# Issuing the loads of later tokens and of the first raw weights behind named stores

## The chip, the cores and the metric

The kernel runs on one core of a Trainium2 chip. A core has four engines that compute, each with its own instruction stream: TensorE (PE in the profile, its weight loads as PEld), VectorE (DVE), ScalarE (ACT) and GpSimdE (POOL). SyncE (SP) issues transfers. A transfer is carried out by the core's 16 DMA engines, and whoever needs its data or its buffer waits for a semaphore. The metric is the device time of one execution in microseconds (us), as a median over runs.

## What is computed

Tokens `x` (2048 x 448, float32) are layer-normalised to `xn`. The output is the sum of three terms: `x`, an attention over `xn`, and a gated feed-forward layer over `xn`.

```python
x = A_x
xn = layernorm(x)
return x + A_ref(xn, wq, wk, wv, wo, beta) + B_ref(xn, w_gate, w_up, w_down)

# A_ref: 16 heads of 28, 4 segments of 512 tokens, one after the other
logits = einsum("bhqd,bhkd->bhqk", qs, ks) * scale + mask
a_dot = softmax(logits) @ vs
a_mem = (phi(qs) @ M) / (phi(qs) @ z + 1e-6)    # phi(t) = t + 1 if t > 0 else exp(t)
o = g * a_mem + (1 - g) * a_dot                 # g = sigmoid(beta), one per head
M = M + phi(ks).T @ vs
z = z + sum(phi(ks))
# then o @ wo

# B_ref
h = sigmoid(xn @ w_gate) * (xn @ w_up)
return h @ w_down
```

So each segment reads the memory `M`, `z` that the segments before it have filled, and attends within itself.

## The kernel before

**Blocks.** The 2048 tokens are worked on in four blocks of 512 (`b` = 0 to 3 in the code, block one to four in the text), which are also the segments. `acc[b]` holds a block's tokens and later collects the output; `xs[b]` holds the normalised, transposed tokens as a high and a low part. Products of full precision are made of 11 TensorE products of such parts.

**The front** (lines 268 to 562) runs over the four blocks. For a block it

- multiplies the four groups of 128 tokens by the value weights (`values`, product `pv`), copies the result into `vst`, and stores that to DRAM as `vd[b]` (L332);
- in the first of these groups, takes the statistics of the *next* block's tokens on VectorE (`statistics`, L285 to L287), which is the first use of `acc[b + 1]`;
- multiplies by seven pieces of the key and query weights (`keys_queries`, product `pp` at L344), the pieces in step `k` = 0 to 6. ScalarE copies each result into a tile `qk` (L345) and makes `e`, that is phi of the keys or queries (L349, L350). VectorE adds the low part (L351), and SyncE stores the tile to `qd[b]` (L352). In later blocks phi of the queries goes to `fd[b]` as well (L357);
- turns phi of the keys with TensorE (`key_rows`, product `pk`, copied to `kn` by ScalarE at L366) and updates the memory (`update`, product `pmm` at L372). The product `pmm` of the first update uses the PSUM bank that the second `pk` used, so it comes after that copy at L366;
- normalises and turns the next block's tokens (`normalise`, and `turn` with the product `pt` at L95);
- reads the memory for the block before (`phi_queries` loads `phi` from `fd`, L383; `recall`, product `n` at L390).

The tiles `qk` come from a pool of four buffers, `four_k`. A fifth tile, and the tiles `hh` of the feed-forward, can be written only when the store of the one that had the buffer has landed. The first buffers of the pool are also used by the raw value weights and one raw piece of the key and query weights.

**The feed-forward** is a generator, `gated`. Each `next(ffn)` lets it issue a few instructions. Its first steps load the first raw weights (`load_up(0)`), split them into a high and a low part (`ready_up(0)`, L85 on ScalarE and L86 on VectorE, into `wgu`), and load the next ones (`load_up(1)`, `load_down(0)`). They are called in the front. Its TensorE products (`pgu` at L240, then `pd` at L166) begin in block four of the front. After the front the feed-forward runs on, and the attention within blocks (`Pair`, `Unit`, products `st` and `pa`) is woven between its steps; that part loads its keys and queries from `qd` (L580) and its values from `vd`.

**What sets the order.** In the front, TensorE, ScalarE and VectorE keep the order in which the code is written:

```python
FRONT = {mybir.EngineType.PE, mybir.EngineType.Activation, mybir.EngineType.DVE}
...
    with tc.tile_pool(name="front", bufs=2) as sb, tc.manual_schedule(engines=FRONT):
```

SyncE is not among them. Its order in the front is made by a scheduler when the program is built, which issues a transfer as soon as it thinks that the transfer is ready; a load into a buffer that nobody has used is ready at once. Within SyncE's queue the order is then fixed: an entry that waits holds up those behind it. After the front, TensorE and SyncE keep the order of the code.

Of the kernel before, what the change touches and what calls it, by code (L numbers as in the profile page):

```python
# [9 lines left out]
F32 = mybir.dt.float32  # L10
# [6 lines left out]
P = 128  # L17
# [44 lines left out]
def kernel(  # L62
# [10 lines left out]
    nc = tc.nc  # L73
# [8 lines left out]
    acc = [keep.tile([P, NT, D], F32, name=f"acc{b}") for b in range(NB)]  # L82
# [5 lines left out]
    def split_weights(w, raw):  # L88
        split(w[:, 0:4, :], w[:, 4:8, :], raw)
# [18 lines left out]
    def x_block(b):  # L108
        return x[b * L:(b + 1) * L, :].rearrange("(t p) d -> p t d", p=P)
# [5 lines left out]
    def bank(name, tag):  # L115
        return ps.tile([P, L], F32, name=name, tag=tag, bufs=banks[tag])
# [17 lines left out]
    qd = [dram.tile([2 * D, 2, L], F32, name=f"qd{b}") for b in range(NB)]  # L134
# [6 lines left out]
    def eight_k(dtype, name):  # L141
        return mid.tile([P, 8, 256], dtype, name=name, tag="8k")

    def four_k(dtype, name):
        return mid.tile([P, 2, L], dtype, name=name, tag="4k", bufs=4)
# [13 lines left out]
    def gated():  # L159
# [14 lines left out]
        def load_up(f):  # L174

            raw_up[f] = mid.tile([P, 1024], F32, name="raw", bufs=2)
            if f < NF:
                nc.sync.dma_start(raw_up[f], w_ffn[f][:, :1024])
            else:
                nc.sync.dma_start(raw_up[f][:, :2 * D], w_o[:, 2 * D * (f - NF):2 * D * (f - NF + 1)])  # L180

        def load_down(f, tag="rawd"):
            raw_down[f] = (mid.tile([P, 1024], F32, name="raw", bufs=2)[:, :D] if tag == "raw" else
                           mid.tile([P, D], F32, name="rawd", bufs=1))
            nc.sync.dma_start(raw_down[f], w_ffn[f][:, 1024:])

        def ready_up(f):
            wgu[f] = eight_k(F32R, "wgu")
            split_weights(wgu[f], raw_up[f].rearrange("p (c n) -> p c n", c=4))
# [10 lines left out]
        load_up(0)  # L200
        yield
        ready_up(0)
        load_up(1)
        load_down(0)
        yield
# [62 lines left out]
    with tc.tile_pool(name="front", bufs=2) as sb, tc.manual_schedule(engines=FRONT):  # L268
# [21 lines left out]
        def root(vh):  # L290
            y = sb.tile([P, vh.shape[1]], F32, name=f"y{vh.shape[1]}")
            A.activation(y, vh, AF.Sqrt, scale=-2.0)
            return y
# [26 lines left out]
        def turn(b, t, xn):  # L320
            transpose_split(bank("pt", "s"), xn, xs[b], t)
# [7 lines left out]
        def store_values(b, t, pv):  # L329
            A.activation(vst[:, t, :, :DH], pv[:, :D].rearrange("p (h d) -> p h d", d=DH), AF.Copy)  # L330
            if t == NT - 1:
                nc.sync.dma_start(vd[b], vst.rearrange("p t h d -> p t (h d)"))  # L332

        def values(b, t):
            pv = bank("pv", "p")
            value_terms(b, t, pv, EARLY[1] if b == 0 else TERMS)
            store_values(b, t, pv)

        def keys_queries(b, c):

            qk = four_k(F32R, "qk")
            pp = bank("pp", ("p", "gu" if b < NB - 1 else "s")[c % 2])
            for n, (a, w) in enumerate(TERMS):
                T.matmul(pp, wqk[c][:, w, :], xs[b][:, a, :], start=n == 0, stop=n == len(TERMS) - 1)  # L344
            A.activation(qk[:, 0, :], pp, AF.Copy)  # L345
            e = None
            if (c < 4 and b < NB - 1) or (c > 2 and b > 0):
                e = sb.tile([P, L], F32, name="e", tag="e", bufs=5)
                A.activation(e, pp, AF.Relu, scale=-1.0)  # L349
                A.activation(e, e, AF.Exp, scale=-1.0)  # L350
            V.tensor_sub(qk[:, 1, :], pp, qk[:, 0, :].bitcast(F32))  # L351
            nc.sync.dma_start(qd[b][c * P:(c + 1) * P], qk.bitcast(F32))  # L352
            if e is not None:
                V.scalar_tensor_tensor(e, pp, 0.0, e, op0=ALU.max, op1=ALU.add)
                if c > 2 and b > 0:
                    lo = max(c * P - D, 0)
                    nc.sync.dma_start(fd[b][lo:(c + 1) * P - D], e[D + lo - c * P:])  # L357
            return e
# [22 lines left out]
        def phi_queries(b, i):  # L381
            phi = sb.tile([GW, L], F32, name="phi", tag="e", bufs=5)
            nc.sync.dma_start(phi, fd[b][i * GW:(i + 1) * GW])  # L383
            return phi

        def recall(b, i, phi):
            ts = sb.tile([P, L], F32, name="ts", bufs=1)
            tb = sb.tile([P, L], F32, name="tb", bufs=2)
            n2 = bank("n2", ("m", "pd")[i % 2])
            T.matmul(n2, mst[b % 2][i], phi, start=True, stop=True)  # L390
            V.transpose(ts, n2)
            weigh(sb, ts, gate[:, i:i + 1], MEM_EPS)
            V.transpose(tb, ts)
            nc.gpsimd.dma_start(od[b][P * i:P * (i + 1)], tb)
# [28 lines left out]
        def split_qk(c):  # L423
            r = raw_qk[c].rearrange("p (c n) -> p c n", c=4)
            A.activation(wqk[c][:, 0:4, :], r, AF.Copy)
            G.tensor_sub(wqk[c][:, 4:8, :], r, wqk[c][:, 0:4, :].bitcast(F32))
# [39 lines left out]
        for t in range(2):  # L466
# [23 lines left out]
                        compare_op=ALU.is_ge, fill=0.0)  # L490

        ffn = gated()
        for b in range(NB):
            last = b == NB - 1
            phi, xn = {}, {}
            if b > 1:
                phi = {i: phi_queries(b - 1, i) for i in range(NG)}
            st = None
            for t in range(3 if b == 0 else 0, NT):
                values(b, t)  # L500
                if b > 1 and t > 0:
                    recall(b - 1, t - 1, phi[t - 1])
                if b == 0:
                    split_qk(t)
                if last:
                    continue
                if t == (3 if b == 0 else 0):
                    mv, vh = statistics(b + 1, 0, NT)
                if t == (3 if b == 0 else 0):
                    st = mv, vh, root(vh)  # L510
                if t == (3 if b == 0 else 2):
                    A.activation(one, ident[:, 0:1], AF.Exp)  # L512
            if st and b > 0:
                st = rstd(*st)
                for n in range(2):
                    xn[n] = normalise(b + 1, n, *st[n])
            e = {}
            for k, c in enumerate((3, 4, 5, 6, 0, 1, 2) if last else range(7)):
                e[c] = keys_queries(b, c)
                if b == 0 and c + 4 < 7:  # L520
                    split_qk(c + 4)
                if k == 0:
                    if b > 1:
                        recall(b - 1, NG - 1, phi[NG - 1])
                    if b == 0:
                        st = rstd(*st)
                    if b < 2:
                        nc.sync.dma_start(acc[b + 2], x_block(b + 2))
                    if b == 0:
                        A.activation(gate, gate, AF.Exp, scale=-1.0)  # L530
                        V.tensor_scalar_add(gate, gate, 1.0)
                        V.reciprocal(gate, gate)
                        V.tensor_scalar(gate_n, gate, -1.0, 1.0, op0=ALU.mult, op1=ALU.add)
                if last:
                    if k > 0:
                        next(ffn)
                    if 2 <= k < 6:
                        phi[k - 2] = phi_queries(b, k - 2)
                    if k > 4:
                        begin[k - 5]()  # L540
                        recall(b, k - 5, phi[k - 5])
                    continue
                if 2 <= k < 6:
                    key_rows(k - 2, e[k - 2])
                if 4 <= k:
                    update(b, k - 4)
                if k == 6:
                    update(b, 3)
                n = k - 1 if b == 0 else k + 1
                if 2 <= n < 6:  # L550
                    turn(b + 1, n - 2, xn[n - 2])
                if 0 <= n < 4 and n not in xn:
                    xn[n] = normalise(b + 1, n, *st[n])
                if b in (1, 2) and k == 5:
                    next(ffn)
            if last:
                for i in range(2):
                    for _ in range(FILLS[i]):
                        next(ffn)
                    if i == 0:  # L560
                        begin[2]()
                    recall(b, i + 2, phi[i + 2])
# [207 lines left out]
    with tc.manual_schedule(engines=MANUAL):  # L770
        next(steps)
        k = sum(FILLS) + 6
# [46 lines left out]
```

## Time and profile before

| | |
|---|---|
| median of 3 runs | 697.93 us (696.47 to 700.5) |
| span of the profiled execution | 697.6 us; the page gives that execution no other time |
| TensorE busy | 690.0 us, 99% |
| VectorE, ScalarE, GpSimdE busy | 570.2, 343.6, 148.5 us |
| moved by the DMA engines | 84.37 MB, 121 GB/s on the mean |
| mean granted TensorE clock | 0.997 |

Times in the profile count from the first instruction. A row of a view in order of time has the start, the duration, the engine, the line and what it writes from what it reads; in brackets stands how long the engine was idle before it, and what ended that. For SyncE (SPq) the duration is that of issuing, not of the transfer. A row of a view by stretches has each engine's busy time with its number of instructions, the clock that TensorE was granted as a share of full speed, the share of time that the 16 DMA engines were busy, and what they moved. The page's row of the DMA engines' share, over the span in 40 equal slices (17.4 us each), in tenths:

```profile
DMA  7833545687222423234323343324242432333342
```

### The profile page before, as it was taken

What the parts mean: (1) busy time and instruction counts of PE and PEld (TensorE: products, weight loads), DVE (VectorE), ACT (ScalarE), POOL (GpSimd) and SP (SyncE); (2) the same over time, 40 slices, a digit from 0 to 9 for tenths busy, and PEclk for the clock granted to TensorE, in tenths of its full rate; (3) what the DMA queues carried; (4) which work ended last, traced back from release to release, by engine and by line L of the source; (5) the groups of instructions that cost most, each with busy time, mean ns of one, the idle gap of its engine ahead of it and who ended that gap; (6) DMA issues with size and microseconds to landing.
All of it is one profiled execution on the core that took longest, in us unless ns stands there. A gap on an engine that the chain in (4) does not pass through costs nothing.

```text
span 697.6 us, 10438 instructions
## 1 busy us (share of the span) xinstructions
PE 690.0 (99%) x3594; PEld 567.7 (81%) x3594; DVE 570.2 (82%) x994; ACT 343.6 (49%) x563; POOL 148.5 (21%) x349
## 2 busy tenths in 40 slices
PE   8989999999999999999999999999999999999997
PEld 7878878777878787877878778787787878778897
DVE  6665687658789898988898889998898889889863
ACT  5646646344455455543655446455644555446320
POOL 4400010101222131322222222132221322222000
PEclk9999999999999999999999999999999999999999
DMA  7833545687222423234323343324242432333342
GB/s 265 320 130 149 201 185 211 226 300 224 70 77 65 120 86 85 48 113 108 78 58 96 70 128 66 98 56 114 74 108 66 95 70 60 86 94 88 91 152 105
DMA packets 45797, 84.37 MB, mean 121 GB/s; under 512 B 6321, under 2 KB 20401, under 8 KB 45233
## 3 DMA queue, kind: packets, MB, share of 16 engines
q1 hardware_dynamic: 42736, 76.37, 35.3%
q0 software_dynamic: 3008, 7.34, 5.2%
q8 instruction: 28, 0.46, 0.3%
q14 instruction: 25, 0.20, 0.1%
HBM read 51.05 MB, written 32.64 MB: 120 GB/s over the span
## 4 chain that ended last, share of the span: by engine, by line
PE 94%; DMA 2%; DVE 1%; ACT 1%; SPq 0%; issue 0%; ACTq 0%
PE pgu L240 42%; PE pd L166 20%; PE pp L344 9%; PE st L597 5%; PE pa L672 5%; PE po L756 5%; PE pv L326 4%; PE pmm L372 2%; PE n L390 1%; DMA qd<-qk 1%; DMA acc<-in_x 1%; PE pt L95 1%; PE pk L364 1%; DVE stats L285 0%; ACT L512 0%
## 5 line engine op out<-in xcount | busy, mean ns | idle before, releaser
L240 PE MATMUL pgu<-xs,wgu 128*128 128x512 f32 x1232 | 321.0, 398 | 0.0
L240 PEld LDWEIGHTS pgu<-xs,wgu 128*128 128x128 f32 x1232 | 226.6, 188 | 48.0 <-issue 3.2
L166 PE MATMUL pd<-wdn,hh 128*128 128x448 f32 x672 | 162.4, 368 | 0.0
L612 POOL TENSOR_SCALAR_AFFINE_SELECT w<-w 128x256 f32<-128x256 f32 (+1 forms) x160 | 81.7, 512 | 254.1 <-ACT w L601 215.1
L166 PEld LDWEIGHTS pd<-wdn,hh 128*128 128x128 f32 x672 | 123.2, 188 | 15.1 <-issue 1.0
L652 ACT ACTIVATE w<-w 128x1024 f32<-128x1024 f32 (+1 forms) x96 | 87.1, 915 | 87.6 <-DVE w L651 87.0
L651 DVE TENSOR_TENSOR w<-w,mb 128x1024 f32<-128x1024 f32 (+1 forms) x96 | 99.7, 1049 | 0.2
L601 ACT ACTIVATE w<-st 128x512 f32<-128x512 f32 x128 | 75.0, 588 | 43.6 <-PE st L597 43.5
L614 DVE TRANSPOSE_TENSOR_REDUCE mx<-w 128x32 f32<-128x1024 f32 x64 | 79.1, 1235 | 12.7 <-POOL w L612 12.7
L344 PE MATMUL pp<-xs,wqk 128*128 128x512 f32 x308 | 80.6, 412 | 0.0
L344 PEld LDWEIGHTS pp<-xs,wqk 128*128 128x128 f32 x308 | 58.1, 192 | 14.8 <-issue 2.4
L169 DVE TENSOR_TENSOR acc<-pd,acc 128x448 f32<-128x448 f32 x112 | 67.4, 602 | 2.7 <-PE pd L166 2.5
L597 PE MATMUL st<-qk 84*128 84x128 f32 (+3 forms) x256 | 64.0, 311 | 0.0
L251 ACT ACTIVATE hh<-sg 128x512 fp32r<-128x512 f32 x56 | 35.1, 627 | 44.5 <-DVE sg L249 35.0
L597 PEld LDWEIGHTS st<-qk 84*128 84x128 f32 x256 | 48.4, 189 | 8.6 <-ACT w L601 0.2
L248 ACT ACTIVATE sg<-pgu 128x512 f32<-128x512 f32 x56 | 33.3, 594 | 40.1 <-PE pgu L240 40.1
L641 DVE STREAM_TRANSPOSE mb<-top 128x1024 f32<-128x1024 f32 x32 | 39.8, 1242 | 10.3 <-POOL top L638 10.1
L351 DVE TENSOR_TENSOR qk<-pp,qk 128x512 fp32r<-128x512 f32 x28 | 19.3, 688 | 34.6 <-ACT e L349 27.3
L249 DVE SCALAR_TENSOR_TENSOR sg<-sg,pgu 128x512 f32<-128x512 f32 x56 | 37.4, 668 | 4.8 <-PE pgu L240 4.8
L252 DVE SCALAR_TENSOR_TENSOR hh<-sg,hh 128x512 fp32r<-128x512 f32 x56 | 38.6, 690 | 2.7 <-ACT hh L251 2.5
L326 PE MATMUL pv<-wv,xs 128*128 128x448 f32 x176 | 39.7, 377 | 0.3
L672 PE MATMUL pa<-w,vv 128*32 128x128 f32 (+3 forms) x512 | 38.4, 436 | 0.0
(100 smaller groups left out, 639.2 us busy)
## 6 DMA issues: line engine op xcount, KB each, us to landing
qk<-qd SPq DMA_DIRECT2D x192, 112.0 KB
qd<-qk SPq DMA_DIRECT2D x28, 512.0 KB
raw<-in_w_ffn SPq DMA_DIRECT2D x14, 512.0 KB
vd<-vst SPq DMA_DIRECT2D x4, 1024.0 KB
vv<-vd SPq DMA_DIRECT2D x16, 256.0 KB
od<-w POOLq DMA_DIRECT2D x16, 256.0 KB, 4.0
sums<-od SPq DMA_DIRECT2D x32, 128.0 KB
out<-acc SPq DMA_DIRECT2D x16, 224.0 KB
```

The lines of the kernel that those rows point to most:

```text
L166: T.matmul(pd[:, :D], l, r, start=n == 0, stop=n == len(mms) - 1)
L169: V.tensor_add(acc[b][:, t, :], pd[:, :D], acc[b][:, t, :])
L240: T.matmul(dst, wgu[f][:, w, side * P:(side + 1) * P], xs[b][:, a, :], start=n == 0, stop=n == len(TERMS) - 1)
L326: T.matmul(pv[:, :D], xs[b][:, a, t * P:(t + 1) * P], wv[w], start=n == 0, stop=n == len(TERMS) - 1)
L344: T.matmul(pp, wqk[c][:, w, :], xs[b][:, a, :], start=n == 0, stop=n == len(TERMS) - 1)
L597: T.matmul(st[:, at:at + L - kb * P], self.qk[:KS, 1, h, kb * P:(kb + 1) * P], self.qk[:KS, 0, h, kb * P:], start=True, stop=True)
L601: A.activation(w, st, AF.Copy)
L612: G.affine_select(d, d, pattern=pattern, base=0, channel_multiplier=-1, compare_op=ALU.is_ge, fill=MASK)
L614: V.tensor_reduce(mx[:, 16 * (n - 1):16 * (n + 1)], w3[:, n // 2, :2 * L].rearrange("p (b n) -> p b n", n=32), axis=mybir.AxisListType.X, ...
L651: V.tensor_sub(w, w, m)
L652: A.activation(w, w, AF.Exp, scale=SCALE)
L672: T.matmul(pa[32 * j:32 * j + 32, kb * P:], self.vv[:, kb, 32 * j:32 * j + 32], self.pairs[j // 2].block(j % 2, kb), start=kb == 0, stop=k ...
```

## The change

Three groups of transfers get a named place in SyncE's queue. `keys_queries` keeps each store to `qd` in a dictionary `stored`, and `tc.issue_after(store)` makes what is traced under it on the same engine come behind that store in the queue. It is an order of issue alone: nothing waits for the store to land.

- The third block's tokens (`acc[2]`) go behind the store of block one's fourth piece, step (0, 3), and the fourth block's (`acc[3]`) behind the store of block two's first, step (1, 0).
- The first raw weights (`load_up(0)`) go behind the store of block three's second piece, step (2, 1).
- `ready_up(0)`, which splits them, becomes a step of its own (a `yield` behind it) and is called at step (2, 6) instead of (2, 5). The loads that came with it, `load_up(1)` and `load_down(0)`, are called at (3, 0), behind the first store of block four.

```diff
@@ gated
         load_up(0)
         yield
         ready_up(0)
+        yield
         load_up(1)
         load_down(0)
         yield
@@ keys_queries
+        stored = {}
+
         def keys_queries(b, c):
...
-            nc.sync.dma_start(qd[b][c * P:(c + 1) * P], qk.bitcast(F32))
+            stored[b, c] = nc.sync.dma_start(qd[b][c * P:(c + 1) * P], qk.bitcast(F32)).ins
@@ the loop over the pieces
                     if b == 0:
                         st = rstd(*st)
-                    if b < 2:
-                        nc.sync.dma_start(acc[b + 2], x_block(b + 2))
...
+                if (b, k) in ((0, 3), (1, 0)):
+                    with tc.issue_after(stored[b, c]):
+                        nc.sync.dma_start(acc[b + 2], x_block(b + 2))
+                if (b, k) in ((2, 1), (3, 0)):
+                    with tc.issue_after(stored[b, c]):
+                        next(ffn)
                 if last:
                     if k > 0:
                         next(ffn)
...
-                if b in (1, 2) and k == 5:
+                if b == 2 and k == 6:
                     next(ffn)
```

The order of TensorE and of GpSimdE stays the same. What moves on SyncE in the front is shown in three places. In the names `acc_71` is `acc[2]`, `acc_72` is `acc[3]`, `qd_78` to `qd_81` are `qd` of block one to four, `vd_86` and so on `vd`, `raw` and `rawd` the raw feed-forward weights, and a number behind x counts equal rows in a run. First SyncE's queue from the end of the first loads to block two, before:

```order
L415 DMA gate<-in_beta 32x4x1 x4
L528 DMA acc_71<-in_x 128x4x448
L528 DMA acc_72<-in_x 128x4x448
L178 DMA raw<-in_w_ffn 128x1024 x2
L332 DMA vd_86<-vst 128x2048
L185 DMA rawd<-in_w_ffn 128x448
L352 DMA qd_78<-qk 128x1024 x7
L332 DMA vd_87<-vst 128x2048
L352 DMA qd_79<-qk 128x1024 x4
```

and after:

```order
L418 DMA gate<-in_beta 32x4x1 x4
L333 DMA vd_86<-vst 128x2048
L355 DMA qd_78<-qk 128x1024 x4
L537 DMA acc_71<-in_x 128x4x448
L355 DMA qd_78<-qk 128x1024 x3
L333 DMA vd_87<-vst 128x2048
L355 DMA qd_79<-qk 128x1024
L537 DMA acc_72<-in_x 128x4x448
L355 DMA qd_79<-qk 128x1024 x3
```

The five loads that stood ahead of the first store to `qd` are gone from there, and the two token loads stand behind the fourth and the eighth store. The raw weights come back further down. SyncE's queue at the beginning of block four, here with the buffers' numbers (`qd3` and `fd3` are block four's), before:

```order
L352 DMA qd3_81<-qk_1372 128x1024
L357 DMA fd3_85<-e_1386 64x512
L352 DMA qd3_81<-qk_1404 128x1024
L357 DMA fd3_85<-e_1418 128x512
L352 DMA qd3_81<-qk_1430 128x1024
L357 DMA fd3_85<-e_1444 128x512
L383 DMA phi_1455<-fd3_85 112x512
L352 DMA qd3_81<-qk_1457 128x1024
```

and after:

```order
L355 DMA qd3_81<-qk_1368 128x1024
L360 DMA fd3_85<-e_1382 64x512
L178 DMA raw_1400<-in_w_ffn 128x1024
L185 DMA rawd_1402<-in_w_ffn 128x448
L355 DMA qd3_81<-qk_1404 128x1024
L360 DMA fd3_85<-e_1418 128x512
L355 DMA qd3_81<-qk_1430 128x1024
L360 DMA fd3_85<-e_1444 128x512
L386 DMA phi_1455<-fd3_85 112x512
L185 DMA raw_1499<-in_w_ffn 128x448
L355 DMA qd3_81<-qk_1457 128x1024
```

A raw load and a down-weight load now follow the block's first stores, and a second down-weight load (`raw_1499`), which stood in block three before, follows the first `phi`. Some rows further on in the same queue, before:

```order
L352 DMA qd3_81<-qk_1483 128x1024
L383 DMA phi_1509<-fd3_85 112x512
L383 DMA phi_1531<-fd3_85 112x512
L352 DMA qd3_81<-qk_1511 128x1024
L185 DMA rawd_1575<-in_w_ffn 128x448
L178 DMA raw_1614<-in_w_ffn 128x1024
```

and after:

```order
L355 DMA qd3_81<-qk_1483 128x1024
L386 DMA phi_1509<-fd3_85 112x512
L355 DMA qd3_81<-qk_1511 128x1024
L386 DMA phi_1531<-fd3_85 112x512
L185 DMA rawd_1575<-in_w_ffn 128x448
L178 DMA raw_1614<-in_w_ffn 128x1024
```

The last `phi`, which came ahead of block four's sixth store, now comes behind it, with the third raw load right behind that `phi`.

On ScalarE the split of the first raw weights moves behind the last piece of block three, before:

```order
L366 ACTIVATE kn<-pk 128x4x64
L85 ACTIVATE wgu<-raw 128x1024
L345 ACTIVATE qk<-pp 128x512
L349 ACTIVATE e<-pp 128x512
L350 ACTIVATE e<-e 128x512
L330 ACTIVATE vst<-pv 128x16x28 x4
```

and after:

```order
L369 ACTIVATE kn<-pk 128x4x64
L348 ACTIVATE qk<-pp 128x512
L352 ACTIVATE e<-pp 128x512
L353 ACTIVATE e<-e 128x512
L85 ACTIVATE wgu<-raw 128x1024
L331 ACTIVATE vst<-pv 128x16x28 x4
```

Its second half on VectorE (L86) moves in the same way, behind the block's last update of the memory.

## The prediction

> **What bounds the kernel now.** I read the page first, then who waited for whom on TensorE, then the order of time around the one long wait, and back from it to what released it. The page:
>
> ```profile
> span 697.6 us, 10438 instructions
> PE 690.0 (99%) x3594; PEld 567.7 (81%) x3594; DVE 570.2 (82%) x994; ACT 343.6 (49%) x563; POOL 148.5 (21%) x349
> PE 94%; DMA 2%; DVE 1%; ACT 1%; SPq 0%; issue 0%; ACTq 0%
> ```
>
> TensorE (PE) is the bound, and 94% of the chain that ended last is its own work. A change that only moves transfers can win nothing but the rest: TensorE's waits, and time in which it runs slowly. The waits of TensorE over the whole span are two:
>
> ```profile
> PE pmm L372 <- ACT kn L366: 2.1, 1, 2.1
> PE warm L431 <- POOL ident masks.py:199: 1.5, 1, 1.5
> ```
>
> The second is the start, which the change doesn't touch. The first lies in block one. TensorE in order of time there, and at the same steps of block two (start, duration, what, idle before it):
>
> ```profile
> 27.92 2.81 PE L344 MATMUL pp<-xs,wqk 128*128 128x512 f32 x11
> ...
> 31.36 2.80 PE L344 MATMUL pp<-xs,wqk 128*128 128x512 f32 x11
> 34.00 0.60 PE L364 MATMUL pk<-ident,e 128*128 128x128 f32 x4
> 36.73 1.13 PE L372 MATMUL pmm<-vst,kn 128*112 128x128 f32 x8 [2.14 <-ACT kn L366]
> 37.70 0.61 PE L95 MATMUL pt<-ident,xn 128*128 128x128 f32 x4
> 38.05 4.37 PE L344 MATMUL pp<-xs,wqk 128*128 128x512 f32 x11
> 42.26 0.60 PE L364 MATMUL pk<-ident,e 128*128 128x128 f32 x4
> ...
> 72.58 0.60 PE L364 MATMUL pk<-ident,e 128*128 128x128 f32 x4
> 73.02 1.04 PE L372 MATMUL pmm<-vst,kn 128*112 128x128 f32 x8
> 73.89 0.60 PE L95 MATMUL pt<-ident,xn 128*128 128x128 f32 x4
> 74.24 2.80 PE L344 MATMUL pp<-xs,wqk 128*128 128x512 f32 x11
> 76.89 0.60 PE L364 MATMUL pk<-ident,e 128*128 128x128 f32 x4
> ```
>
> In block one TensorE stands still at 34.6, and the eleven products that follow at 38.05 take 4.37 us where the same eleven take 2.80 in block two. Here is what it waits for, first on ScalarE (ACT), then in the chain of work, then on the queue of SyncE (SP) that issues the loads and stores:
>
> ```profile
> 30.00 0.57 ACT L366 ACTIVATE kn<-pk 128x512 f32<-128x512 f32 x1
> 34.45 0.60 ACT L345 ACTIVATE qk<-pp 128x512 fp32r<-128x512 f32 x1 [3.87 <-DMA qd<-qk]
> 36.10 0.58 ACT L366 ACTIVATE kn<-pk 128x512 f32<-128x512 f32 x1
> ```
> ```profile
> 25.08 9.27 DMA qd<-qk
> ```
> ```profile
> 13.23 1.09 SPq L528 DMA_DIRECT2D acc<-in_x  x2
> 16.26 4.32 SPq L178 DMA_DIRECT2D raw<-in_w_ffn  x2
> 20.70 0.65 SPq L332 DMA_DIRECT2D vd<-vst  x1
> 21.39 0.74 SPq L185 DMA_DIRECT2D rawd<-in_w_ffn  x1
> 25.08 5.46 SPq L352 DMA_DIRECT2D qd<-qk  x3
> 39.36 0.32 SPq L352 DMA_DIRECT2D qd<-qk  x1
> ```
>
> ScalarE wants to write block one's fourth `qk` tile into a buffer whose first tile is still being stored to `qd`. That store was issued at 25.08 and took 9.27 us, because 2 x 896 KB of tokens, 2 x 512 KB and 224 KB of raw weights, and 1024 KB of values stand in the queue ahead of it. None of these tokens and raw weights is used before block two (its row at 50.49 stands below). The transfers and the clock by stretches (busy of PE, PEld, DVE, ACT, POOL, then the granted clock, share of the DMA engines, GB/s):
>
> ```profile
> 20.00:34.00 14.00, 14.00 (x69) 11.35 (x67) 8.63 (x20) 9.82 (x19) 7.13 (x8) 1.00 0.93 367
> 38.10:41.60 3.50, 3.50 (x11) 2.76 (x10) 2.68 (x6) 0.64 (x2) 0.47 (x2) 0.51 0.46 183
> 42.00:44.00 2.00, 2.00 (x19) 1.88 (x17) 0.91 (x2) 0.87 (x2) 0.00 (x0) 1.00 0.00 0
> 48.00:690.00 642.00, 642.00 (x3353) 526.86 (x3352) 539.49 (x918) 317.12 (x508) 132.46 (x324) 1.00 0.39 112
> ```
>
> The DMA engines are full from 20 to 34. A store without that crowd, the one issued at 39.36, is over before 42.00, since nothing at all moves from 42 to 44: at most 2.64 us against 9.27. TensorE's clock is granted at 0.51 from 38.1 to 41.6, just after the standstill. From 48 to 690 TensorE has no idle time and the full clock, so a microsecond won before 48 is kept to the end, and there is nothing else to win.
>
> **The change, part by part.** *The loads leave the front.* With them gone only the values' store (1024 KB) stands ahead of the first `qd` store. At the 367 GB/s of the full stretch that is 2.9 us, from 20.70 to about 23.6, before the `qd` store is issued; the latter lands 2.64 us after 25.08, near 27.7 (estimate). ScalarE wants the buffer when the products end, 27.92 + 2.81 = 30.73. So its 3.87 us of waiting go. What is late next? From the `qk` copy to the end of the `kn` copy ScalarE needs 36.10 + 0.58 - 34.45 = 2.23 us; begun at 30.75, that ends at 32.98. TensorE arrives at its `pmm` at 34.00 + 0.44 (block two's step, 73.02 - 72.58) = 34.44. The margin is 1.46 us, so TensorE waits for nothing: the store may even land as late as 32.2.
>
> The gain, by starts in block one less the same steps in block two: `pk` to `pmm` 2.73 - 0.44 = 2.29 us; `pmm` to `pt` 0.97 - 0.87 = 0.10; `pp` to `pk` 4.21 - 2.65 = 1.56, the half clock. Together 3.95 us. The last term needs the clock to fall because of the standstill; without that link the gain is 2.39.
>
> [...] I take 3.95.
>
> *The third block's tokens* now go out behind the store of block one's fourth `qk`, about 33. 896 KB at 367 GB/s are 2.5 us, with a store's 2.64 added some 38.5. VectorE (DVE) first reads them for its statistics:
>
> ```profile
> 50.49 0.63 DVE L285 BATCH_NORM_STATS2 stats<-acc 128x6 f32<-128x448 f32 x1
> ```
>
> less 3.95 that is 46.5, a margin of 8 us, nearly another 9.27 us store. The load shares the engines with the stores of the fifth to seventh `qk`, whose buffers are wanted only in block two. Cost 0; from below it can't gain, since the tokens were there before. *The fourth block's tokens* have all of block two ahead of their use: 0.
>
> *Raw weights.* The first 512 KB load goes behind a store of block three, and its split one step later on ScalarE and VectorE. That step falls in idle time:
>
> ```profile
> 117.31 1.23 DVE L86 TENSOR_TENSOR wgu<-raw,wgu 128x1024 fp32r<-128x1024 f32 x1
> 122.13 0.55 ACT L330 ACTIVATE vst<-pv 128x448 f32<-128x448 f32 x1 [2.21 <-PE pv L326]
> 125.20 0.72 DVE L391 STREAM_TRANSPOSE ts<-n 128x512 f32<-128x512 f32 x1 [3.50 <-PE n L390]
> 148.09 1.05 ACT L85 ACTIVATE wgu<-raw 128x1024 fp32r<-128x1024 f32 x1
> ```
>
> 1.05 us on ScalarE against 2.21 idle, and 1.23 on VectorE against 3.50: 0. The second 512 KB and the first 224 KB of the down weights go behind block four's first store, and another 224 KB load behind `phi`. That is the crowded place:
>
> ```profile
> 136.00:146.00 10.00, 10.00 (x44) 8.08 (x43) 5.91 (x11) 5.08 (x9) 0.54 (x1) 1.00 0.70 255
> 150.00:170.00 20.00, 20.00 (x81) 14.93 (x80) 16.85 (x32) 6.71 (x12) 1.62 (x3) 1.00 0.96 287
> ```
> ```profile
> 144.08 1.07 SPq L383 DMA_DIRECT2D phi<-fd  x1
> 153.38 0.77 SPq L178 DMA_DIRECT2D raw<-in_w_ffn  x1
> ```
> ```profile
> 151.84 1.02 PE L390 MATMUL n<-phi,mst 112*128 112x512 f32 x2
> 158.88 1.04 ACT L85 ACTIVATE wgu<-raw 128x1024 fp32r<-128x1024 f32 x1
> 161.17 1.02 PE L390 MATMUL n<-phi,mst 112*128 112x512 f32 x2
> 168.79 0.40 PE L597 MATMUL st<-qk 84*128 84x512 f32 x1
> ```
>
> 0.98 MB more at 255/0.70 = 364 GB/s are 2.7 us of full engines, and 136 to 146 leaves 0.30 x 10 = 3.0 us free. It fits, barely, and the engines are full after 150. Queued behind the moved loads on SyncE are block four's `qk` stores and the `phi` loads; TensorE waits for `phi` at 151.84 (issue over by 145.15, so 6.7 us to land) and last at 161.17, whose load now stands behind one more store. The third raw load is issued some 0.4 us later, behind that `phi`; ScalarE takes it at 158.88, 4.7 us after its issue ended, and that one may be late by a microsecond. ScalarE then has 9.9 us until TensorE's first `st` at 168.79. On TensorE the cost is between 0 (a store's 2.64 us fits every one of these) and, if `phi` took the front's 9.27 us, 9.27 - 6.7 = 2.6 us of standstill with 1.56 of half clock. The engines were 0.93 full for 14 us in the front, and here they still have 3.0 us free before `phi`: nearer the first. I take 0.
>
> **Sum.** 697.60 - 3.95 = 693.65 for the profiled execution. The page gives it no time but the span; the runs' median 697.93 is 0.33 above it, so 694.0.
>
> **The rivals.** *The clock stays low* for its own reasons somewhere in these 3.5 us: gain 2.39, time 695.5. [...] Against it: no other slow stretch.
>
> *Slower: `phi` late in block four.* The raw loads ahead of it fill the engines, and TensorE stands at the `n` product of 151.84. Each microsecond of lateness costs one, plus 1.56 for the clock. It gives back the 3.95 when the standstill passes 2.4 us, which is a landing 9.1 us after issue; at the front's 9.27 us the sum is 697.93 - 3.95 + 2.6 + 1.6 = 698.2. Over 0.5% slower (3.5 us) takes a standstill near 5.9 us, a landing 12.6 us after issue, longer than anything in the front. Against it: 3.0 us of free engine time.
>
> *It doesn't do what it says.* The first `qd` store is still late, because the values' store alone holds it, or another buffer is waited for: nothing gained, 697.9. Against it: the store would have to land after 32.2, 7.1 us after issue, with one transfer ahead instead of six.
>
> **Chances.** 0.5% (3.5 us) is about what a measurement of this kernel can tell from no change. The forecast gets 0.68; with the runs' own spread (696.47 to 700.5) it lies so near that bound that 0.15 of it counts as within. Clock stays: 0.14, within. `phi` late: 0.10, half of it slower, half within. No effect: 0.08, within, with 0.02 of it slower. Faster 0.53, within 0.40, slower 0.07. The range reaches down by the distance of the fastest run from the median, 694.0 - 1.5 = 692.5, and up past the clock rival and half of the way back, to 697.0; the likeliest case alone is 692.5 to 695.0.
>
> **What would show it.** Right: no wait of ScalarE's L345 copy (L348 after) for `qd` near 30, no TensorE wait for `kn`, block one's sixth `pp` at 2.8 us, granted clock 1.00 from 38 to 42, block two's first `pv` near 44.7 instead of 48.66, the full DMA stretch cut after the front. Wrong: a TensorE wait at `n` or `st` between 130 and 175, VectorE waiting for `acc`, or the half clock at another place.

## The result, and the profile after

The changed kernel takes 695.47 us (median of 18 runs, 695.16 to 695.91). The kernel before takes 696.98 us over 18 runs (696.11 to 700.5), the three shown above among them. The ratio is 0.9975, with a 95% interval of 0.9967 to 0.9983: 0.25% faster, 1.5 to 1.7 us, where 3.9 us were forecast. The time lies within the stated range, 692.5 to 697.0, but the gain is below 0.5%, where the prediction had put its greatest chance on more. As striking as the median is the scatter, 0.75 us after and 4.4 us before.

The page of the profiled execution after:

```profile
span 693.8 us, 10446 instructions
PE 97%; DMA 1%; DVE 1%; SPq 0%; ACT 0%; issue 0%
```

Its own time was 695.5 us, so 1.7 us lie around the span. The waits of TensorE, all of them:

```profile
PE warm L434 <- POOL ident masks.py:199: 1.5, 1, 1.5
PE pv L327 <- DVE xs L102: 0.3, 1, 0.3
PE pt L95 <- DVE xn L312: 0.2, 1, 0.2
```

The wait of `pmm` for the `kn` copy is gone; what is left belongs to the start. Block one on TensorE in order of time, and the start of block two's `pv`:

```profile
33.98 0.60 PE L367 MATMUL pk<-ident,e 128*128 128x128 f32 x4
34.41 1.04 PE L375 MATMUL pmm<-vst,kn 128*112 128x128 f32 x8
35.28 0.60 PE L95 MATMUL pt<-ident,xn 128*128 128x128 f32 x4
35.64 2.80 PE L347 MATMUL pp<-xs,wqk 128*128 128x512 f32 x11
...
44.70 5.66 PE L327 MATMUL pv<-wv,xs 128*128 128x448 f32 x27
```

`pk` to `pmm` takes 0.43 us instead of 2.73, the sixth `pp` 2.80 instead of 4.37, and `pv` begins at 44.70 instead of 48.66. ScalarE at the fourth `qk` copy, and the same stretches of the transfers and the clock:

```profile
30.74 0.60 ACT L348 ACTIVATE qk<-pp 128x512 fp32r<-128x512 f32 x1 [0.19 <-PE pp L347]
```
```profile
20.00:34.00 14.00, 14.00 (x68) 11.33 (x68) 10.47 (x23) 12.51 (x24) 7.10 (x8) 1.00 0.51 206
38.10:41.60 3.50, 3.50 (x25) 3.13 (x24) 1.70 (x4) 1.47 (x3) 0.23 (x1) 1.00 0.60 237
```

The copy no longer waits for a store, only 0.19 us for its own products; the DMA engines are 0.51 full instead of 0.93, and the granted clock from 38.1 to 41.6 is 1.00 instead of 0.51. Between the two profiled executions the span fell by 3.8 us, as the sum had it (697.6 to 693.65; 693.8 came). The runs' medians fell by 1.5. So the question is not where the gain went in the kernel, but which execution of the kernel before the sum was made against.

### The profile page after: what moved, and what is told of

It is laid out like the page before. It is cut to its first block, busy times and chain, and to the rows that moved or that the text cites. A ratio compares the mean times of both kernels' runs of the same rounds, so it can differ in the third digit from the quotient of the medians.

```text
span 693.8 us, 10446 instructions
## 1 busy us (share of the span) xinstructions
PE 688.1 (99%) x3594; PEld 565.7 (82%) x3594; DVE 570.4 (82%) x994; ACT 344.0 (50%) x563; POOL 147.7 (21%) x349
## 4 chain that ended last, share of the span: by engine, by line
PE 97%; DMA 1%; DVE 1%; SPq 0%; ACT 0%; issue 0%
PE pgu L241 42%; PE pd L166 20%; PE pp L347 10%; PE st L604 6%; PE pa L679 5%; PE po L763 5%; PE pv L327 4%; PE pmm L375 2%; PE n L393 1%; DMA acc<-in_x 1%; PE pt L95 1%; PE pk L367 1%; DVE stats L286 0%; DVE acc L767 0%; DVE xs L102 0%
## 5 line engine op out<-in xcount | busy, mean ns | idle before, releaser
L347 PE MATMUL pp<-xs,wqk 128*128 128x512 f32 x308 | 79.0, 405 | 0.0
```

## The experiments

**The kernel before, once more, with span and clock of every execution.** No edit. Theory A says that the profiled execution of before was one of its longer ones; theory B that its span was usual and that the time around the span differs.

> The kernel before, unchanged, for the span and the clock of each execution. Theory A (the profiled execution of before was one of the slow tail): what lies around the span is the same 1.7 us as for the changed kernel, so the spans scatter from about 694.4 to 698.8 with a median near 695.3 (697.0 less 1.7); the mean clock is 1.000 in most executions and 0.997 only in those of span about 697 and more; a profile of a usual execution shows TensorE waiting 1.0 to 1.8 us for the kn copy and no half clock. Theory B (the profiled span was usual, and the time around the span is longer in the changed kernel): spans near 697.6 with times near 697.0 to 698, clock 0.997 in most, half clock in the profile again.

The median was 697.4 us over 12 runs, ratio 1.0001 (0.9984 to 1.0019), from 695.95 to 700.71. What lies around the span is 1.64 to 1.77 us in every execution, so theory B falls: 697.6 us of span belongs to a time of 699.3, and I had set it beside a median of 697.93. With the kernel's runs beside the other experiments there are 83 executions with span and clock. 71 have a mean clock of 0.999 or 1.000 and spans of 694.0 to 696.8; 12 have 0.995 to 0.998 and spans of 697.4 to 700.0; none lies between. The median span is 695.6. The profile before, with 697.6 us and 0.997, belongs with the 12. This run's profile is of the 71:

```profile
core 0: 694.7 us, clock 1.000
```
```profile
PE pmm L372 <- ACT kn L366: 0.7, 1, 0.7
```
```profile
35.24 1.13 PE L372 MATMUL pmm<-vst,kn 128*112 128x128 f32 x8 [0.69 <-ACT kn L366]
36.21 0.60 PE L95 MATMUL pt<-ident,xn 128*128 128x128 f32 x4
36.56 2.81 PE L344 MATMUL pp<-xs,wqk 128*128 128x512 f32 x11
```
```profile
32.96 0.60 ACT L345 ACTIVATE qk<-pp 128x512 fp32r<-128x512 f32 x1 [2.42 <-DMA qd<-qk]
```

The same wait at the same place, but 0.69 us instead of 2.14, and the eleven products after it take 2.81 us instead of 4.37. This execution is 0.9 us of span above the changed kernel, and a usual one 1.8 (695.6 less 693.8). I had expected 1.0 to 1.8 us of waiting in a usual execution; the profiled one is faster than the median, and no profile here is of an execution at the median itself.

**The tokens alone, the raw weights alone.** The first kernel has only the token loads behind the named stores, and the raw weights early as before:

```diff
-                    if b < 2:
-                        nc.sync.dma_start(acc[b + 2], x_block(b + 2))
...
+                if (b, k) in ((0, 3), (1, 0)):
+                    with tc.issue_after(stored[b, c]):
+                        nc.sync.dma_start(acc[b + 2], x_block(b + 2))
```

> Only the two token loads are moved behind the named stores; the raw feed-forward weights are loaded early as before, ahead of the first qd store. Theory A: 1.8 MB less stand ahead of that store, about 4.5 us of full engines, so it lands near 30 and nobody waits: the time of the changed kernel, 695.5, clock 1.000. Rival C (the raw weights next to the store are what makes it late): a wait of 1 us or more stays on TensorE, 696.5 or more. Theory D (the gain comes from the later split of the raw weights or from block four, not from the front): 697.0.

The second is the changed kernel with the token loads put back:

```diff
+                    if b < 2:
+                        nc.sync.dma_start(acc[b + 2], x_block(b + 2))
...
-                if (b, k) in ((0, 3), (1, 0)):
-                    with tc.issue_after(stored[b, c]):
-                        nc.sync.dma_start(acc[b + 2], x_block(b + 2))
```

> Only the raw weights are moved, with the split one step later; the third and fourth block's tokens are loaded early as before. Theory A: 1.27 MB less ahead of the first qd store, about 3.2 us of full engines, which is more than the 2.2 us by which it landed too late in the profiled execution of before (34.4 against 32.2): at most a few tenths of waiting, 695.5 to 695.8. Rival C: 695.5 as well, and e2 slower. Theory D: 695.5.

Measured: 695.54 us (695.46 to 695.68), ratio 0.9975 (0.9964 to 0.9985), and 695.51 (695.39 to 695.61), ratio 0.9973 (0.9962 to 0.9983). Each half does the whole: the changed kernel has 695.47. The store must be early enough, and more than early enough wins nothing. With the raw weights alone moved, it only just is in the profiled execution:

```profile
31.02 0.60 ACT L348 ACTIVATE qk<-pp 128x512 fp32r<-128x512 f32 x1 [0.39 <-DMA qd<-qk]
```

ScalarE still waits 0.39 us for the store, inside the 1.46 us of margin, and TensorE doesn't notice. Rival C (the raw weights are what makes it late) and theory D (the gain comes from elsewhere) fall.

**No transfer moved, but a buffer of its own.** The kernel before, in which the fourth `qk` tile of block one takes an idle buffer of another pool:

```diff
-            qk = four_k(F32R, "qk")
+            if (b, c) == (0, 3):
+                qk = eight_k(F32R, "qk_own").rearrange("p (a m) n -> p a (m n)", a=2)[:, :, :L]
+            else:
+                qk = four_k(F32R, "qk")
```

> No transfer is moved. Block one's fourth qk tile gets a buffer of its own (one that the raw key and query weights have left), so that its ScalarE copy doesn't wait for the first qd store; all loads stay early. Theory A: the standstill is gone though the store is as late as before: 695.5 to 695.8, and the profile shows the first qd store still taking 7 us or more. If the gain of the change came from lighter traffic itself (TensorE, ScalarE or VectorE working faster beside fewer transfers), the time stays at 697.0.

695.5 us (695.25 to 695.95), ratio 0.9969 (0.9955 to 0.9983). The crowd is as it was, and the copy doesn't wait:

```profile
20.00:34.00 14.00, 14.00 (x68) 11.34 (x68) 10.34 (x23) 12.52 (x24) 7.09 (x8) 1.00 0.95 378
```
```profile
30.79 0.60 ACT L348 ACTIVATE qk_own<-pp 128x512 fp32r<-128x512 f32 x1 [0.25 <-PE pp L347]
```

By the semaphore's updates in the trace the first `qd` store, issued at 25.04, landed at 33.1, 8.1 us later. That is later than the 32.2 which the prediction allows, and the time is still that of the changed kernel. So the gain is the buffer's wait; lighter traffic adds nothing to it that these runs show. All ten executions have a clock of 0.999 or 1.000: without the standstill none of these ten has the half clock, though the transfers are the same.

**More ahead of the store.** The kernel before with 896 KB copied to a scratch in DRAM, between the token loads:

```diff
                         nc.sync.dma_start(acc[b + 2], x_block(b + 2))
+                    if b == 0:
+                        nc.sync.dma_start(spare, x[0:L, :])
```

> The kernel before with one transfer more in the front: 896 KB of tokens copied from DRAM to a DRAM scratch that nobody reads, issued between the two token loads (the scheduler puts the 224 KB load of raw down weights behind the first qd store in exchange, so net some 0.7 MB more ahead of it). Theory A: the first qd store lands 1.7 us later or more, near 34.5 to 36 in a usual execution, and TensorE stands still 2.3 to 4 us. The time has two parts: the standstill, and the half clock after it, now in most executions. 698.5 to 702 median, most mean clocks at 0.998 or below, and again a wide scatter. Rival E (the half clock has nothing to do with the standstill): the time grows by the standstill alone, 698.5 to 699.5, and the mean clock stays 0.999 to 1.000 in most executions.

701.04 us (698.87 to 702.44), ratio 1.0041 (1.0022 to 1.0059) against 697.61 beside it. Nine of ten executions have a mean clock of 0.998 or below. In the profiled one:

```profile
24.95 10.08 DMA qd<-qk
```
```profile
PE pmm L373 <- ACT kn L367: 2.9, 1, 2.9
```
```profile
37.42 2.05 PE L373 MATMUL pmm<-vst,kn 128*112 128x128 f32 x8 [2.94 <-ACT kn L367]
```
```profile
37.20:40.50 3.30, 3.08 (x13) 3.03 (x14) 2.66 (x6) 1.77 (x5) 0.24 (x1) 0.50 0.40 163
```

The price has the two parts that were expected, 2.94 us of standstill and a clock of 0.50 behind it, and rival E falls. The store takes 10.08 us here, against 9.27 in the profile before, which is of a long execution, and 8.1 with the buffer of its own.

**What makes the crowd so late.** Before, the DMA engines are hardly used just ahead of the full stretch, though transfers wait in the queue:

```profile
16.00:20.00 4.00, 4.00 (x23) 3.70 (x22) 2.93 (x9) 2.70 (x6) 2.29 (x2) 1.00 0.26 85
```
```profile
8.69 4.17 SPq L415 DMA_DIRECT2D gate<-in_beta  x4
13.23 1.09 SPq L528 DMA_DIRECT2D acc<-in_x  x2
```

Four loads of `beta`, each 128 values of 4 bytes over 32 partitions, take SyncE 4.17 us to issue. The tokens behind them are issued by 14.32, so from 16 to 20 the engines don't lack issued work; of the 466 packets that the trace has in these 4 us, 278 are of 4 bytes. This kernel leaves them out and sets the gate to zero, so the sigmoid of beta is not computed:

```diff
-            for j in range(HG):
-                nc.sync.dma_start(gate[32 * j:32 * j + 32], beta[j::HG].partition_broadcast(32))
+        G.memset(gate, 0.0)
```

> The kernel before without the four small loads of beta (512 values of 4 bytes each, repeated over partitions) that stand right ahead of the token loads in the queue; the gate is set to zero on GpSimdE instead, so beta's part of the computation is left out. The scheduler also puts the 224 KB load of raw down weights ahead of the values' store. All other early loads stay. In before, the DMA engines moved only 27 to 130 KB per us from 16 to 20, with the small loads in flight and the token loads behind them. Theory G (the small loads hold the engines, and so make the crowd late and its end uncertain): the full stretch begins 2 to 4 us earlier, the first qd store lands before 31, no standstill: 695.5 with a scatter below 1 us. Theory H (the small loads only wait in the same queue; the 5 MB alone make the store late): 696.5 to 697.5 with the scatter of before.

695.7 us (695.64 to 696.03), ratio 0.9975 (0.9963 to 0.9986): the time of the changed kernel, with every early load in place. The same stretch, and the queue:

```profile
16.00:20.00 4.00, 4.00 (x23) 3.70 (x22) 2.94 (x8) 2.86 (x6) 2.15 (x2) 1.00 1.06 384
```
```profile
8.72 2.29 SPq L526 DMA_DIRECT2D acc<-in_x  x2
```

384 GB/s instead of 85. The tokens are issued at 8.72 instead of 13.23, and by the semaphore's updates the first `qd` store lands at 29.1. So it takes both to make the store late: 2 KB of tiny pieces, and the whole 4.2 MB (4064 KB; the expectation's 5 MB is too much) that stands between them and the store. With the tiny pieces goes most of the scatter (0.4 us against 2.8 for the kernel before beside it). How much of the lateness is the issuing and how much the pieces in flight was not separated.

**Block four's margin.** The prediction put the cost there at nothing and the fit at bare. The changed kernel with 896 KB copied to a scratch right behind the moved raw loads:

```diff
                         next(ffn)
+                        if b == 3:
+                            nc.sync.dma_start(spare, x[0:L, :])
```

> The changed kernel with 896 KB more of idle copying (DRAM to a DRAM scratch) issued in block four, right behind the moved raw loads and ahead of the phi loads. It tries the margin that the prediction called bare. Theory A with the prediction's margins: 0.9 MB more are 2.5 us of full engines where 0.3 us were thought to be left, so phi is some 2.2 us later against a margin of about 4 us beyond a plain store: no wait of TensorE at n, 695.5 to 695.8. Rival F (block four is already at its edge in the changed kernel): a wait at n or st, 697 or more.

701.2 us (699.77 to 703.48), ratio 1.0043 (1.0026 to 1.006) against the kernel before: the expectation was wrong, and the place is tight. In the profiled execution, of 700.23 us, TensorE waits at the attention's first products, and seven of the ten executions have a mean clock of 0.997 or below:

```profile
PE st L607 <- ACT w L611: 1.9, 1, 1.9
PE st L607 <- DMA qk<-qd: 0.8, 1, 0.8
```

Then half of the copy (`spare[0:L // 2]`, `x[0:L // 2, :]`):

> The changed kernel with 448 KB of idle copying in block four, half of the run before this one. There the fd stores landed some 4.7 us later, TensorE just did not wait at n and waited 0.8 us for the first pair of the attention. If half the copy means half the delay, 2.3 us, every margin of block four (3.7 us at the first phi, 3.7 at the first pair) holds: 695.5 to 695.8, no wait of TensorE. If a wait shows, the margin left by the change is below 2.3 us: 696.5 or more.

697.16 us (695.38 to 699.34), ratio 0.9997 (0.9983 to 1.0011): the whole gain of the change is lost in the usual execution. Its profile was of the fastest one and shows no wait. The same kernel twice more:

> The same kernel as the run with half the copy, for the profile of a more usual execution (its times went from 695.4 to 699.3, and the one profiled was the fastest). If the margin that is exceeded is phi's, TensorE waits at n (L394) for phi; if it is the first pair's, it waits at st (L607) for the qk load, as with the whole copy. 0.5 to 2.5 us of wait in a span of 694.5 to 696.5.

> The same kernel once more, for a second such profile; the same expectation.

They took 696.01 and 697.26 us, single runs, with 0.4 and 1.8 us of TensorE waiting at `st` for a copy of ScalarE's. First the one's wait, then the other's:

```profile
PE st L607 <- ACT w L611: 0.4, 1, 0.4
```
```profile
PE st L607 <- ACT w L611: 1.8, 1, 1.8
```

and ScalarE there, first in the changed kernel, then in these two executions in the same order:

```profile
155.40 1.06 ACT L85 ACTIVATE wgu<-raw 128x1024 fp32r<-128x1024 f32 x1 [0.41 <-DMA raw<-in_w_ffn]
```
```profile
157.48 1.06 ACT L85 ACTIVATE wgu<-raw 128x1024 fp32r<-128x1024 f32 x1 [1.48 <-DMA raw<-in_w_ffn]
```
```profile
157.19 0.58 ACT L85 ACTIVATE wdn<-rawd 128x448 fp32r<-128x448 f32 x1 [2.90 <-DMA rawd<-in_w_ffn]
158.93 1.06 ACT L85 ACTIVATE wgu<-raw 128x1024 fp32r<-128x1024 f32 x1 [1.16 <-DMA raw<-in_w_ffn]
```

With half the copy, neither `phi` nor the first pair is the tight place, as my expectations had it, but the loads that ScalarE splits ahead of the attention: in the second of these executions it stands 2.90 us at a down-weight load and 1.16 at the third raw load behind it. With the whole copy the first pair is late as well, by the 0.8 us above. The third load's split is 2.08 us later than in the changed kernel where TensorE waits 0.4 us, and 3.53 us later where it waits 1.8. So what the change leaves of margin is 1.7 us, counted from the 155.40 of the changed kernel, which already holds 0.41 us of waiting. Rival F (already at the edge) is wrong by this 1.7 us; TensorE waits at `n` in none of the profiles with a copy.

## Why the prediction was right, and where it was not

- *The front's chain* (store late, buffer, `qk` copy, `kn` copy, `pmm`) was right; the own buffer shows it with the transfers untouched, and the wait is gone in the profile after.
- *The gain of 3.95 us* was right for the execution that was profiled and too large for the usual one. The step that failed is the last of the sum: "The page gives it no time but the span; the runs' median 697.93 is 0.33 above it". The distance around the span is 1.7 us in every execution of both kernels, so that span stood for 699.3, 2.3 us above the median over 18 runs. The usual execution has 1.8 us to win by the spans (695.6 to 693.8), a shorter standstill without the half clock, and that came. That the result still lies in the range is partly luck: the likeliest case alone, 692.5 to 695.0, misses it, and the range reached up to 697.0 for the sake of rivals that didn't hold. The spread of the three runs, 4 us, was in hand; I read it as the measurement's noise, and it was mostly the wait itself, of a different length in each execution: the four kernels that remove it scatter by 0.2 to 0.75 us.
- *The half clock*, 1.56 us of the 3.95, occurs, by the mean clock, in 12 of 83 executions of before. That it comes from the standstill was right: none in 48 executions of the four kernels that remove the wait (the changed one, tokens alone, raw weights alone, own buffer; at most 0.001 off full), against 9 of 10 when it is longer; and 7 of 10 when TensorE stands still in block four instead. That it belongs to the usual price was wrong. *The clock rival* had the result's time, 695.5, by a mechanism that doesn't hold: it keeps the half clock, and the changed kernel has none (1.00 from 38.1 to 41.6 in its profile, a mean clock of 0.999 or 1.000 in all 18 executions).
- *Third and fourth block's tokens, first raw weights: 0.* Right: TensorE waits for none of them, and VectorE begins the statistics without a wait, at the 46.5 that was forecast:

```profile
46.52 0.63 DVE L286 BATCH_NORM_STATS2 stats<-acc 128x6 f32<-128x448 f32 x1
```

- *Block four: 0, barely.* Right in the sum (the profiled span, 693.8, is that of the own buffer, which moves no transfer), wrong in the margin. The 9.9 us granted to ScalarE "until TensorE's first `st`" overlook what stands between in its queue (`sg` and `hh` of the feed-forward; in the profile after, the two `hh` there wait 3.75 and 2.70 us for VectorE); 1.7 us are there. *The rival of a late `phi`* named the right crowd and the wrong victim.
- *No effect* fell with the first profile after. *The chances* put 0.53 on a gain of over 0.5% and 0.40 on a result within it; the gain is 0.25%.

## What to carry to other kernels

Before a sum is made against a profile, find out which execution it is: compare its span, plus what lies around it, with the runs, and treat a scatter of the runs as a wait of uncertain length, not as noise. A wait on a buffer can be taken away at the buffer, at the loads, or at what slows the loads; each alone was worth the same here (695.47 to 695.7 us), since all that counted was that the copy into the buffer didn't hold up TensorE. Loads that are moved out of one crowd should be followed to the queue of the engine that uses them next, item by item, for the margin there is what that queue leaves.

## What the hardware showed that I had not expected

In the profile before, with four loads of 2 KB in all in the queue, the 16 DMA engines move 85 GB/s for 4 us while 1.8 MB of issued tokens wait behind them; without these loads it is 384.

Whether the half clock comes doesn't seem to hang on the length of the standstill alone. In the profile before, 2.14 us of waiting were followed by a granted clock of 0.51 from 38.1 to 41.6. Yet 71 executions of that kernel kept a mean clock of 0.999 or more with spans up to 696.8, which is 3.0 us above the changed kernel's. If all of that is standstill (an estimate; no profile here is of such an execution), 3.0 us of it went without the half clock that followed the 2.14.

Two profiles with a copy in block four lie close together. A standstill of 1.88 us (the whole copy) is followed by a granted clock of 0.50, and one of 1.84 us (half the copy) by one of 1.00. The rows are the standstill's end and the stretch behind it, first with the whole copy, then with half:

```profile
171.58 0.50 PE L607 MATMUL st<-qk 84*128 84x512 f32 x1 [1.88 <-ACT w L611]
```
```profile
172.10:175.40 3.30, 3.30 (x9) 2.68 (x9) 1.75 (x2) 0.89 (x2) 0.70 (x3) 0.50 0.23 84
```
```profile
170.38 0.50 PE L607 MATMUL st<-qk 84*128 84x512 f32 x1 [1.84 <-ACT w L611]
```
```profile
172.50:175.80 3.30, 3.30 (x17) 2.90 (x16) 1.52 (x4) 0.91 (x2) 0.00 (x0) 1.00 0.02 5
```

The two standstills differ by 0.04 us. What besides the length decides was not shown.
